# Block-sparse attention and a feed-forward layer on one core: first batch with fixed keys and fixed v blocks used from one place, sampled keys copied for both halves of the heads at once, and the third tile's neighbour blocks loaded from memory

## Chip, core, metric

The kernel runs on 1 core of one Trainium2 chip. The metric is the device time of one execution in microseconds (us); lower is better. The kernel before was timed three times.

## What is computed

Four batches, 8 heads, 768 rows of 64 numbers; the rows lie in 24 blocks of 32. A block of queries sees its own block and its two neighbours, the first and the last block of the keys, and three sampled blocks. The first and the last block of queries see everything. A feed-forward layer follows, over all 3072 tokens of width 512. All is f32.

```python
def _attn_ref(q, k, v, sampled_blocks):            # q, k, v: 4, 8, 768, 64
    scores = scale * np.matmul(q, k.transpose(0, 1, 3, 2))
    mask = np.abs(blk_i - blk_j) <= 1
    mask = mask | (blk_i == 0) | (blk_j == 0) | (blk_i == n_blocks - 1) | (blk_j == n_blocks - 1)
    for qb in range(n_blocks):
        for kb in sampled_blocks[qb]:
            mask[qb * block:(qb + 1) * block, kb * block:(kb + 1) * block] = True
    scores = np.where(mask, scores, -1000000000.0)
    ...
    return np.matmul(attn, v)

def _moe_ref(x, w_in, w_out):                      # 3072 x 512, 512 x 2048, 2048 x 512
    h = np.maximum(x @ w_in, 0.0)
    return h * h @ w_out
```

## The kernel before

A **tile** is 128 rows of queries (4 blocks) of one batch: 24 tiles, numbered k = 0 to 23, six a batch (t = 0 to 5). Three tiles make a **chunk**; the feed-forward layer works on a chunk at a time (`moe`), while the attention of the next chunk runs between its matmuls. The first chunk (k = 0, 1, 2) has no such partner: its attention is all there is in the first 58 us, and we call this stretch **the start**. `moe(0)` begins when the three tiles of x are done: `turn` turns them (tile xt), casts (xh, on ACT) and takes the rest (xl, on DVE), and the first product of the layer is ph<-xh,WI (L788).

The attention is cut into units. A `Half` is one tile and half of the heads (u = 0 or 1): `scores` (tile s, L374), `maxima` (m, DVE, L385), `exps` (p, ACT, L423), `turn` (pt, PE, L437), `copies` (pT, ACT, L446), `values` (pv, PE, L459) and `norm` (x, DVE, L474 to L479). A `Whole` does the first and last block of queries of a batch for a pair of heads (tiles g, mg, pg, ptg, pTg, pvg, in the same steps). In the start there are 4 wholes and 6 halves, put in by `units` one every STEP_0 = 5 steps, and a table of lags (LAG_0) says how many steps lie between two parts of a unit. Every engine then works through its own list in this written order, and an instruction that waits holds up all that stand behind it on its engine.

What a Half needs beside q:

- **Keys.** kn holds all keys of the batch for one half of the heads. KG holds, for one tile, the fixed blocks (first and last) and three sampled blocks for each of its four blocks of queries. For batch 0, POOL fills KG: `static_keys` (L284) one copy of 128x512 for each half, `copy_keys` (L263) 12 copies of 128x64 for each half. For later batches SP loads KG from memory.
- **v.** Each tile k < 3 has its own V[k]: V[k][0] holds on its first 64 rows the fixed blocks, four times over (once for each block of queries), and below them two sampled blocks; V[k][1] holds the third sampled block and the three neighbours. `load_sampled` (L317) brings the sampled blocks with 12 DMAs a tile on SP's queue. The fixed blocks are loaded once and copied five times (`copy_static`, L209, ACT). The neighbours of k = 0 are loaded; those of k = 1 and 2 are copied from vn, the batch's v (`copy_window`, L217, 24 copies of 32x260 a tile), on POOL, ACT and DVE.

SP's DMAs take eight semaphores in turn, so that one is issued only when the eighth before it has landed. On POOL's queue lie the loads of kn and vn and of the feed-forward weights (craw, L692, 512 KB each), AHEAD = 5 of them ahead of their use: the weights come as 64-bit numbers, and a `cut` (L708, L710 on ACT, L719, L720 on DVE) makes f32 of a craw.

```python
        if now >= FIXED_0 and fixed:
            f, *at = fixed.pop(0)
            f(*at, nc.scalar.copy)          # one ACT copy a step, from step 7 on
        if now >= CUT_0[0] and (now - CUT_0[0]) % CUT_0[1] == 0:
            cut_next()                      # one weight block every 5 steps, from step 30 on
```

## Time and profile before

| | us |
|---|---|
| time, median of 3 runs (758.05 to 761.56) | 760.67 |
| time of the profiled execution | 760.55 |
| its span, first to last instruction | 758.8 |
| attention of the first chunk until the first xh | 58.0 |
| busy in the span: PE / ACT / POOL / DVE | 732.4 / 539.7 / 502.3 / 499.8 |

The span is taken from one execution. Its own time is 1.75 us longer than the span; that part lies around the first and last instruction. A group line gives the line of the kernel, engine, operation, the tiles out<-in, the shape and the count, then busy time and mean ns of one, then the engine's idle time just before them and what ended it. In the timeline the columns are start, length (of all instructions in the row together), engine, line and operation. PEld is the loading of weights into TensorE; SPq and POOLq are DMA issues. The view of windows gives busy time of every engine in a stretch, then the granted TensorE clock, the busy share of the DMA engines and GB/s.

### The profile page before, as it was taken

The page shows a single profiled execution, that of the slowest core. Times are in us where ns is not written, and L with a number is a line of the kernel's source. Part 1 is how long each engine was busy: PE and PEld are TensorE (multiplying, and loading weights), DVE is VectorE, ACT ScalarE, POOL GpSimd, SP SyncE. Part 2 cuts the span into 40 slices and gives each one's busy share as a digit, 9 for nine tenths or more (in the row PEclk, how much of TensorE's full clock was granted, in tenths as well). Part 3 has the DMA queues.
Part 4 walks back from the last instruction along what each step waited for, and adds up shares of the span by engine and source line. Part 5 has one row for each costly group of instructions (what it writes and reads, how often), then busy time and mean ns, then how long its engine had stood idle before and what let it go on. Part 6 is the DMA issues. An engine that isn't in the chain of part 4 may idle for free.

```text
span 758.8 us, 26292 instructions
## 1 busy us (share of the span) xinstructions
PE 732.4 (97%) x9832; PEld 612.3 (81%) x9832; DVE 499.8 (66%) x987; ACT 539.7 (71%) x1193; POOL 502.3 (66%) x636
## 2 busy tenths in 40 slices
PE   4879999999999999999999999999999999999997
PEld 2656776668888888888888888887888888888986
DVE  5785785658785756667777575666868666645452
ACT  5896877798876876789786767679876776733222
POOL 6963844227776675757767567666876575777885
PEclk9799999999999999999999999999999999999999
DMA  8776799544543536544434344655344352201001
GB/s 283 224 215 172 228 264 344 130 117 131 140 114 93 146 86 176 153 109 128 113 105 106 101 126 109 221 120 140 79 124 118 75 143 64 51 1 44 1 1 41
DMA packets 92290, 97.45 MB, mean 128 GB/s; under 512 B 14787, under 2 KB 79428, under 8 KB 92164
## 3 DMA queue, kind: packets, MB, share of 16 engines
q1 hardware_dynamic: 86036, 72.41, 37.1%
q0 software_dynamic: 5696, 22.58, 9.2%
q8 instruction: 78, 1.28, 0.7%
q10 hardware_dynamic: 432, 0.79, 0.3%
q14 instruction: 48, 0.39, 0.2%
HBM read 89.43 MB, written 6.29 MB: 126 GB/s over the span
## 4 chain that ended last, share of the span: by engine, by line
PE 85%; ACT 5%; DMA 4%; DVE 4%; issue 1%; SPq 1%; ACTq 0%; POOL 0%; DVEq 0%; POOLq 0%
PE ph L788 33%; PE po L826 30%; PE s L374 7%; PE pv L459 5%; PE po L816 4%; PE g L546 2%; PE pvg L604 2%; DMA V<-in_v_dram 2%; DMA KG<-in_k_dram 1%; PE xt L773 1%; PE pt L437 1%; DVE xl L777 1%; ACT V L209 1%; DMA kn<-in_kn_dram 1%; SPq L317 1%
## 5 line engine op out<-in xcount | busy, mean ns | idle before, releaser
L413 ACT ACTIVATE pm<-p 32x256 f32<-32x256 f32 x576 | 239.2, 415 | 13.2 <-DVE p L391 4.8
L788 PE MATMUL ph<-xh,wi 128*128 128x384 f32 x832 | 237.8, 347 | 0.0
L826 PE MATMUL po<-wo,gh 128*128 128x512 f32 x672 | 213.8, 399 | 0.0
L755 POOL TENSOR_TENSOR wi<-W,wi 128x512 fp32r<-128x512 f32 x104 | 142.3, 1368 | 68.4 <-DVE wi L754 35.2
L806 POOL TENSOR_TENSOR gl<-gf,gh 128x384 fp32r<-128x384 f32 x112 | 117.4, 1048 | 93.0 <-DVE gf L804 80.6
L755 POOL TENSOR_TENSOR wo<-WO,wo 128x512 fp32r<-128x512 f32 x112 | 145.9, 1302 | 49.5 <-DVE wo L754 48.5
L792 ACT ACTIVATE r<-ph 128x384 f32<-128x384 f32 x128 | 63.0, 492 | 161.3 <-PE ph L788 156.1
L804 DVE SCALAR_TENSOR_TENSOR gf<-ph,r 128x384 f32<-128x384 f32 x112 | 62.3, 556 | 150.3 <-ACT r L792 136.4
L788 PEld LDWEIGHTS ph<-xh,wi 128*128 128x128 f32 x832 | 150.4, 188 | 13.4 <-issue 7.4
L826 PEld LDWEIGHTS po<-wo,gh 128*128 128x128 f32 x672 | 123.5, 188 | 23.0 <-issue 2.8
L788 PE MATMUL ph<-xl,wi 128*128 128x384 f32 x416 | 141.4, 340 | 0.0
L826 PE MATMUL po<-wo,gl 128*128 128x512 f32 x336 | 133.2, 396 | 0.0
L754 DVE CAST wo<-WO 128x512 fp32r<-128x512 f32 x112 | 84.4, 753 | 0.0
L788 PEld LDWEIGHTS ph<-xl,wi 128*128 128x128 f32 x416 | 78.2, 188 | 6.9 <-issue 2.9
L826 PEld LDWEIGHTS po<-wo,gl 128*128 128x128 f32 x336 | 63.1, 188 | 15.7 <-POOL gl L806 1.0
L385 DVE TENSOR_REDUCE m<-s 128x2 f32<-128x512 f32 x96 | 61.6, 683 | 11.2 <-PE s L374 10.9
L799 ACT ACTIVATE gh<-r 128x384 fp32r<-128x384 f32 x112 | 59.0, 526 | 9.3 <-ACT r L792 0.4
L459 PEld LDWEIGHTS pv<-V,pT 128*32 128x32 f32 x3072 | 47.7, 110 | 19.8 <-issue 9.5
L459 PE MATMUL pv<-V,pT 128*32 128x65 f32 x3072 | 56.2, 223 | 5.0 <-ACT pT L446 4.8
L788 PE MATMUL ph<-xh,WI 128*128 128x384 f32 x192 | 54.4, 344 | 0.8 <-ACT xh L776 0.8
L374 PE MATMUL s<-KG,q 64*32 64x160 f32 x1536 | 51.2, 305 | 1.4 <-issue 1.0
L418 DVE STREAM_TRANSPOSE pT<-pm 128x1024 f32<-128x1024 f32 x36 | 44.6, 1239 | 4.9 <-ACT pm L413 4.7
(85 smaller groups left out, 933.0 us busy)
## 6 DMA issues: line engine op xcount, KB each, us to landing
craw<-in_w_dram POOLq DMA_DIRECT2D x32, 512.0 KB, 5.9
V<-in_v_dram SPq DMA_DIRECT2D x504, 32.5 KB, 1.8
KG<-in_k_dram SPq DMA_DIRECT2D x216, 64.0 KB, 2.0
V<-in_v_dram SPq DMA_DIRECT2D x28, 390.0 KB, 4.5
q<-in_q_dram SPq DMA_DIRECT2D x24, 256.0 KB, 3.0
out_dram<-ot SPq DMA_DIRECT2D x21, 256.0 KB, 2.5
V<-in_v_dram SPq DMA_DIRECT2D x16, 292.5 KB, 4.2
vn<-in_vn_dram SPq DMA_DIRECT2D x5, 780.0 KB, 6.4
```

The source lines that it names most:

```text
L374: nc.tensor.matmul(self.sb[e][j * BLK : (j + 1) * BLK, i * NSLOT + a : i * NSLOT + z], q[r, j, pr, :], k, start=True, stop=True,)
L385: nc.vector.tensor_reduce(m[:, e], self.sb[e].rearrange("p (i c) -> p i c", i=2), axis=AX, op=ALU.max)
L413: nc.scalar.activation(p[a * BLK : (a + 1) * BLK, j], x[j * BLK : (j + 1) * BLK, :, a], AF.Exp, scale=SCALE)
L459: nc.tensor.matmul(po[j * BLK : (j + 1) * BLK, h * VW : (h + 1) * VW], self.pT[:, j, 2 * e + i, c], v[:, self.u, j, hv : hv + VW], start=( ...
L754: nc.vector.tensor_copy(w[:, 0], src)
L755: nc.gpsimd.tensor_tensor(w[:, 1], src, w[:, 0], op=ALU.subtract)
L788: nc.tensor.matmul(ph[:, :TOK], w, x, start=(i == 0), stop=(i == len(steps) - 1))
L792: nc.scalar.activation(r, ph[:, :TOK], AF.Relu)
L799: nc.scalar.activation(gh, r, AF.Square)
L804: nc.vector.scalar_tensor_tensor(gf, ph[:, :TOK], 0.0, r, op0=ALU.max, op1=ALU.mult)
L806: nc.gpsimd.tensor_tensor(gl, gf, gh, op=ALU.subtract)
L826: nc.tensor.matmul(acc[c][u], g[:, at], w[:, k], start=(f == 0 and i == 0), stop=(f == NF - 1 and i == 2))
```

## The change

Five things, all for the first batch.

1. **Fixed keys from one place.** KG of tiles in batch 0 holds the sampled blocks alone. The scores against the first and last block are taken straight from the keys, for all 128 queries of the tile in one matmul per head (128x64). For this q is laid out so that a head's 128 queries lie side by side. `static_keys` is gone for these tiles.
2. **Fixed blocks of v from one place.** A tile `fixed` (64 rows, both halves) is loaded once. In `values` of tiles k < 3 one matmul per head multiplies it for all 128 queries; the sampled part of V[k][0] is multiplied from row 64 down. The six ACT copies of `copy_static` are gone; for tile 3 the fixed blocks are loaded (64x4x260, two DMAs). The turned p (pT) is laid out so that a head's 128 columns lie side by side.
3. **Both halves at once.** The keys lie in one tile KN and v in one tile VN; a sampled block is copied for both halves by one POOL copy (128x128), but for tile 0. Neighbour blocks of tile 1 are copied for both halves by one copy (32x2x260): 8 on POOL, 4 on ACT, none on DVE.
4. **Third tile.** The neighbours of tile k = 2 are loaded from memory by two DMAs, ahead of its sampled blocks on SP's queue.
5. **Order.** STEP_0 is 4, with new lags; the first half of tile 0 stands after two wholes instead of four; `values` of the start take their PSUM bank from the other pool; AHEAD is 4.

```diff
-AHEAD = 5
+AHEAD = 4
-STEP_0 = 5
+N_0 = 1
+STEP_0 = 4
+FROM_MEMORY = (2,)
-LAG_0 = {"s": 2, "x": 2, "t": 3, "c": 2, "v0": 2, "n": 2}
+LAG_0 = {"s": 3, "x": 2, "t": 3, "c": 1, "v0": 3, "n": 2}
-FIXED_0 = 7
-ON_ACT = 12
+FIXED_0 = 22
+ON_POOL, ON_DVE = 8, 0
...
-        copy(V[k][1][(1 + n) * BLK : (2 + n) * BLK, i, j], st["vn", b, i][r : r + BLK, blk // NJ])
+        copy(V[k][1][(1 + n) * BLK : (2 + n) * BLK, :, j], st["vn"][r : r + BLK, :, blk // NJ])
...
-        for u in range(2):
-            if t < UC:
-                static_keys(b, t, u, nc.gpsimd.tensor_copy)
-            kn = st["kn", b, u]
+        for us in (slice(0, 1), slice(1, 2)) if t == 0 else (slice(0, 2),):
             for j in range(NJ):
                 for r in range(NRAND):
                     nc.gpsimd.tensor_copy(
-                        kg[:, j, 2 + r, 2 * u : 2 * u + 2].unsqueeze(1), kn[:, bass.ds(vals[NRAND * j + r], 1)]
+                        k5[:, j, r, us].unsqueeze(2), KN[:, us, bass.ds(vals[NRAND * j + r], 1)]
                     )
...
+                for e in range(2 if b == 0 else 0):
+                    r = slice(e * D, (e + 1) * D)
+                    to = self.sb[e][:, i * NSLOT : i * NSLOT + S_RAND]
+                    nc.tensor.matmul(to, q[r, pr].rearrange("p j s -> p (j s)"), kn[r, 0 : NBLK : NBLK - 1, i, :], start=True, stop=True)
...
+            for e, i, at in heads:
+                h = e, i, at
+                if e:
+                    self.products(po, h, 0, VA, 2 * BLK, True, False)
+                    self.products(po, h, 1, VB, 0, False, False)
+                p = self.pT[0 : 2 * BLK, 2 * e + i, 0].rearrange("p j q -> p (j q)")
+                nc.tensor.matmul(po[:, at], p, st["fixed"][:, self.u, at], start=e == 0, stop=e == 1)
+                if e == 0:
+                    self.products(po, h, 1, VB, 0, False, False)
+                    self.products(po, h, 0, VA, 2 * BLK, False, True)
...
-                if self.t == NT - 1:
+                if self.t in (0, NT - 1) and (self.t or self.b == 0):
                     load_static(n, self.u)
...
+            whole = wholes[:2] + halves[:N_0] + wholes[2:] + halves[N_0:]
+            return [(i * STEP_0, u) for i, u in enumerate(whole)]
...
+    st["fixed"] = rot.tile([P, NT, HW // 2], F32, tag="vn", name="fixed", bufs=1)[0 : 2 * BLK, 0:2]
+    nc.sync.dma_start(st["fixed"].rearrange("p u c -> p (u c)"), vd[0, V_STATIC * BLK :])
+    for k in FROM_MEMORY:
+        load_window(k, None)
```

What this does to the engines' lists is seen at three places. ACT's list from its first exponential on (names end in whole or tile, half and a number of the buffer; pg, pTg belong to wholes, p and pT to halves, V to tiles' v). Before:

```order
L562 ACTIVATE pg_0_443<-g_0_0_434,mg_0_438 128x512
L562 ACTIVATE pg_0_443<-g_0_1_435,mg_0_438 128x256
L209 COPY V_78<-V_78 64x780 x2
L209 COPY V_122<-V_78 64x1040
L592 COPY pTg_0_466<-ptg_0_0_451 128x512
L562 ACTIVATE pg_1_469<-g_1_0_446,mg_1_459 128x512
L562 ACTIVATE pg_1_469<-g_1_1_447,mg_1_459 128x256
L209 COPY V_122<-V_78 64x1040
L209 COPY V_124<-V_78 64x1040 x2
L217 COPY V_125<-vn_0_133 32x260 x2
```

ACT's list of the changed kernel, from the second whole's exponentials to the four copies of neighbour blocks:

```order
L574 ACTIVATE pg_1_468<-g_1_1_408,mg_1_414 128x256
L604 COPY pTg_1_513<-ptg_1_0_501 128x512
L420 ACTIVATE p_0_0_474<-s_0_0_0_427,m_0_0_471 128x256 x2
L420 ACTIVATE p_0_0_474<-s_0_0_1_428,m_0_0_471 128x256 x2
L443 COPY pT_0_0_573<-pt_0_0_0_559 128x512
L443 COPY pT_0_0_573<-pt_0_0_1_560 128x512
L574 ACTIVATE pg_2_576<-g_2_0_509,mg_2_529 128x512
L574 ACTIVATE pg_2_576<-g_2_1_510,mg_2_529 128x256
L604 COPY pTg_2_704<-ptg_2_0_628 128x512
L574 ACTIVATE pg_3_707<-g_3_0_569,mg_3_586 128x512
L574 ACTIVATE pg_3_707<-g_3_1_570,mg_3_586 128x256
L211 COPY V_124<-VN 32x2x260 x4
```

The copies of V that stood between the wholes are gone; the first half's p and pT stand before the third whole, and the copies that are left stand behind the fourth whole's exponentials.

PE's list before, at the values of tile 0's first half (pv_0_0), which stand behind the scores of tile 1 (s_1_0):

```order
L374 MATMUL s_1_0_0_832<-KG_94,q_1_143 32x160
L374 MATMUL s_1_0_1_833<-KG_94,q_1_143 32x160
L459 MATMUL pv_0_0_868<-V_78,pT_0_0_815 32x65 x4
L459 MATMUL pv_0_0_868<-V_79,pT_0_0_815 32x65 x4
L459 MATMUL pv_0_0_868<-V_78,pT_0_0_815 32x65 x4
```

PE's list of the changed kernel at the same values:

```order
L616 MATMUL pvg_1_534<-VN,pTg_1_513 32x65 x24
L434 MATMUL pt_0_0_0_559<-ident,p_0_0_474 128x128 x4
L434 MATMUL pt_0_0_1_560<-ident,p_0_0_474 128x128 x4
L558 MATMUL g_3_0_569<-KN,QG 128x512
L558 MATMUL g_3_1_570<-KN,QG 128x256
L462 MATMUL pv_0_0_591<-fixed,pT_0_0_573 128x65
L472 MATMUL pv_0_0_591<-V_79,pT_0_0_573 32x65 x4
L472 MATMUL pv_0_0_591<-V_78,pT_0_0_573 32x65 x8
```

They now stand ahead of the third whole's turning, of the scores of tile 0's second half and of all of tile 1, and they read V_78 and V_79, into which the 12 sampled DMAs of tile 0 write.

SP's list before, from the last sampled DMA of tile 1 to the first ones of tile 2 (ISA rows are address arithmetic):

```order
L317 DMA V_123<-in_v_dram 32x2x260
L242 DMA q_2_219<-in_q_dram 128x512
L231 TENSOR_LOAD idx
L317 ISA
L317 DMA V_124<-in_v_dram 32x2x260
```

And of the changed kernel:

```order
L309 DMA V_124<-in_v_dram 32x2x260
L239 DMA q_2_217<-in_q_dram 128x512
L296 DMA V_126<-in_v_dram 96x4x260 x2
L228 TENSOR_LOAD idx
L309 ISA
L309 DMA V_125<-in_v_dram 32x2x260
```

Two DMAs of 390 KB have come in ahead of tile 2's sampled blocks. From the second batch on the lists of all engines are the same as before but for names.

More of the change, by code (lines that the diff above doesn't have):

```diff
@@ L195, in load_static, with copy_window @@
     def load_static(k, u, eng=nc.sync):
-        us = halves(k, u)
-        if us is None:
-            return
-        n = 1 if k == 0 else NJ
-        for i in range(us.start, us.stop):
-            src = columns(vd[order[k][0], V_STATIC * BLK :], i)
-            src = src.unsqueeze(1).broadcast_to([2 * BLK, n, HW // 2])
-            eng.dma_start(values_of(k)[0][0 : 2 * BLK, i, 0:n], src)
-    def copy_static(k, i, copy):
-        src = V[0][0][0 : 2 * BLK, i, 0:1]
-        dst = V[k][0][0 : 2 * BLK, i, 1 if k == 0 else 0 :]
-        copy(dst, src.broadcast_to(list(dst.shape)))
-    def copy_window(k, i, j, n, copy):
+        src = columns(vd[order[k][0], V_STATIC * BLK :], u)
+        src = src.unsqueeze(1).broadcast_to([2 * BLK, NJ, HW // 2])
+        eng.dma_start(values_of(k)[0][0 : 2 * BLK, u], src)
+    def copy_window(k, j, n, copy):
         b, t = order[k]
@@ L248, in keys_of @@
         st["kg", b, t] = (
-            own.tile([P, NJ, 2 + NRAND, NPAIR, BLK], F32, name=f"KG{k}") if own else KG[(k - (k >= UC)) % 2]
+            own.tile([P, NJ, NRAND, NPAIR, BLK], F32, name=f"KG{k}") if own else KG[(k - (k >= UC)) % 2]
         )
```

95 lines of the change are left out of this document (48 added, 47 removed).

## The prediction

> **What bounds the kernel now.** First the page's busy times, then the view of windows with the start (from ACT's first exponential to its last cut before xh) and the rest apart:
>
> ```profile
> PE 732.4 (97%) x9832; PEld 612.3 (81%) x9832; DVE 499.8 (66%) x987; ACT 539.7 (71%) x1193; POOL 502.3 (66%) x636
> 10.42:57.74 47.32, 35.90 (x1047) 27.62 (x1046) 36.48 (x99) 44.78 (x91) 37.92 (x137) 0.89 0.82 234
> 60.00:758.70 698.70, 691.16 (x8772) 581.46 (x8771) 457.41 (x867) 491.68 (x1098) 458.64 (x475) 1.00 0.44 118
> ```
>
> PE's 97% is an average of two stages. After 60 us PE is busy for 691 of 699 us: nothing else can end that stage sooner, and it moves as a block with its beginning. In the start PE is busy for 36 of 47 us, ACT for 44.78. So the start is ACT's, and the time changes by what the first ph moves. Its end, from the timeline:
>
> ```profile
> 55.21 1.25 ACT L446 COPY pT<-pt 128x512 f32<-128x512 f32 x2
> 56.03 1.38 PE L459 MATMUL pv<-V,pT 128*32 128x65 f32 x64 [0.97 <-ACT pT L446]
> 57.88 0.42 DVE L479 TENSOR_TENSOR x<-pv,rec 128x256 f32<-128x256 f32 x1
> 58.03 1.56 ACT L776 CAST xh<-xt 128x512 fp32r<-128x512 f32 x3 [0.29 <-PE xt L773]
> 59.64 0.44 PE L788 MATMUL ph<-xh,WI 128*128 128x384 f32 x1 [0.78 <-ACT xh L776]
> ```
>
> The last copies of pT end at 56.46, and 3.18 us later, through pv, norm, xt and xh, the first ph begins. What ACT does from 10.42 on, in groups:
>
> ```profile
> L217 ACT COPY V<-vn 32x260 f32<-32x260 f32 x24 | 9.7, 406 | 0.4
> L423 ACT ACTIVATE p<-s,m 128x256 f32<-128x256 f32 x24 | 9.7, 530 | 0.1
> L446 ACT COPY pT<-pt 128x512 f32<-128x512 f32 x12 | 7.0, 662 | 2.0 <-PE pt L437 1.9
> L710 ACT ACTIVATE craw<-craw,below 128x512 int32<-128x512 uint16 x6 | 5.2, 873 | 0.0
> L209 ACT COPY V<-V 64x1040 f32<-64x1040 f32 x4 | 4.0, 1062 | 0.0
> L562 ACT ACTIVATE pg<-g,mg 128x512 f32<-128x512 f32 x4 | 2.8, 688 | 8.4 <-DVE mg L555 8.4
> L592 ACT COPY pTg<-ptg 128x512 f32<-128x512 f32 x4 | 2.3, 583 | 0.1
> L708 ACT ACTIVATE W<-craw 128x512 f32<-128x512 f32 x3 | 2.3, 763 | 0.0
> L562 ACT ACTIVATE pg<-g,mg 128x256 f32<-128x256 f32 x4 | 1.9, 468 | 0.0
> L209 ACT COPY V<-V 64x780 f32<-64x780 f32 x2 | 1.6, 836 | 0.0
> ```
>
> **What ACT loses.** The six copies of fixed blocks: 4.0 + 1.6 = 5.6 us. The 24 copies of neighbours: 9.7 us. Four copies of 32x520 come in. No such copy is in the trace; it lies between 32x260 (0.41) and 64x780 (0.84), and I take the middle, 0.63, so 2.5 us. A step count from the new lags ends the start with five cuts instead of six: one cut (0.76 + 0.87, of which ACT overlaps some) is 1.3 us. In all 5.6 + 9.7 - 2.5 + 1.3 = 14.1 us. If nothing else stood in the way, the first ph would move by that much. It is the upper end of the gain.
>
> **What is late next: the sampled blocks of tile 0.** pv_0_0 now stands on PE ahead of the third whole's turning and of the second half's scores, and it needs all 12 sampled DMAs of tile 0. Its list before that is short: after the first ptg, at 12.1, come s_0_0, pvg, ptg, g, pvg, pt, g, and by the rows
>
> ```profile
> 11.25 0.85 PE L584 MATMUL ptg<-ident,pg 128*128 128x128 f32 x6 [0.37 <-ACT pg L562]
> 14.43 0.89 PE L604 MATMUL pvg<-vn,pTg 128*32 128x65 f32 x48 [1.00 <-ACT pTg L592]
> 15.96 1.46 PE L546 MATMUL g<-kn,QG 128*128 128x512 f32 x4
> 36.83 1.09 PE L437 MATMUL pt<-ident,p 128*128 128x128 f32 x8
> 84.74 1.14 PE s L374 x62
> ```
>
> they take 1.14 + 0.89 + 0.85 + 1.46 + 0.89 + 1.09 + 1.46 = 7.8 us. So PE stands at pv_0_0 at about 20. When is the data there? In SP's timeline and the DMA view (the last two rows are one DMA issued at 20.74, and the span of all those of L317 in the first 60 us):
>
> ```profile
> 8.21 13.10 SPq L317 DMA_DIRECT2D V<-in_v_dram  x12
> 17.85 2.18 POOL L263 COPY KG<-kn 128x64 f32 x12
> 19.98 2.61 POOL L692 DMA_DIRECT2D craw<-in_w_dram  x5
> V<-in_v_dram SPq DMA_DIRECT2D x1, 65.0 KB, 5.9
> DMA to landing us min/median/max: 2.2/4.5/9.8
> ```
>
> The twelfth was issued at 20.74 and landed 5.9 us later, at 26.6. Nobody minded: pv_0_0 ran at 34.9. The five craw loads share its way. In the changed kernel POOL has three copies of 0.61 less ahead of them, and its second dozen pairs become one dozen of 128x128 (0.18 for 64 elements, 0.61 for 512: about 0.25 each), so the loads, now four, go out at about 16.9 instead of 19.98. SP's pace up to the eighth DMA (17.7) stays, since it waits for landings of loads that are the same as before. So at about 19, when weights begin to flow, five of the twelve are still to come. How fast they go beside weights, in the DMA view from 22 to 30 us:
>
> ```profile
> q0 software_dynamic: 655, 2.41, 86.8%
> q1 hardware_dynamic: 406, 0.34, 14.4%
> ```
>
> q1 is SP's: 0.34 MB in 8 us are 5.1 DMAs of 65 KB, 1.56 us each. Five take 7.8 us, to 26.8. I take 26.7. Bounds: with the shortest landing of that row, 20.7 + 2.2 = 22.9; with the longest, 30.5. So a **new wait of PE of some 6.7 us**, for everything behind pv_0_0 on its list, takes the place of ACT's copies, and ACT runs dry behind it.
>
> The Trainium skill, "DMA: Bandwidth & Descriptors", section on queues, rings and completion order, states that each DMA engine takes turns between its queues packet by packet. The counts above (655 to 406, the latter 1 KB each) lean that way but are not equal; with strictly equal turns q1's five DMAs would be through sooner, by about 23, and that is the first rival below.
>
> **From the wait to the first ph.** Clock rows:
>
> ```profile
> 26.58:29.99 3.41, 1.22 (x50) 0.64 (x36) 3.20 (x11) 3.35 (x9) 3.27 (x11) 1.00 1.04 345
> 29.99:33.40 3.41, 2.83 (x42) 2.33 (x48) 3.16 (x12) 1.49 (x4) 3.41 (x18) 0.50 0.76 172
> 31.15 1.97 PE L437 MATMUL pt<-ident,p 128*128 128x128 f32 x8
> ```
>
> After 3.4 us with PE mostly idle the granted clock was 0.50, and eight transposes took 1.97 instead of 1.09 us. I expect the same behind the new wait. So from 26.7: two thirds of pv_0_0 and four transposes of ptg, 1.25 us at full clock, some 2.2 at half; ACT gets work at 28.9. The skill's page "TensorE: Matmul & The Clock Gate", part 1, gives the rule (about 3.4 us of idle bring half rate) and the row agrees; without it the time would be 1 us less.
>
> What ACT then does is compared with a stretch of before:
>
> ```profile
> 33.77 1.57 ACT L423 ACTIVATE p<-s,m 128x256 f32<-128x256 f32 x4
> ```
>
> From here (p of the second half) to the end of the last pT at 56.46 ACT took 22.7 us with five halves, seven neighbour copies, five cuts, a cast and its waits. The changed list from 28.9 on has the same five halves and cast, four cuts (-1.3), no such copies (-2.9), and in addition two pTg (0.58 each), one whole's exponentials (4.7 / 4 = 1.18) and the four wide copies (2.5), less the tenth by which such rows overlap on ACT (the groups above add up to more than 44.78): 4.45. That is 22.7 - 1.3 - 2.9 + 4.45 = 23.0, to 51.9. The tail of 3.18 us loses about 0.3, since pv now has 36 matmuls instead of 64 (1.38 us). First ph at about 54.8 instead of 59.64: **4.8 us less**.
>
> **Edits that I cost at nothing.** DVE was busy for 36.5 of the start's 47 us and loses all its neighbour copies. POOL was busy for 37.9 of them, and its copies of sampled keys for tiles 1 and 2 halve in number; they were hidden behind ACT, and stay so behind the wait. Were DVE as late as ACT, the cover would be gone, and each half's norm would add its own time; nothing in the rows says so. The two DMAs of fixed blocks for tile 3 fall into the stretch before 60, where the DMA engines have slack (0.82 busy). In the second chunk PE is the bound, and scores with 96 instead of 160 columns save at most 0.1 us of 1.14 for each of six halves; I count 0.3, inside the error. The sum goes against the profiled execution's own 760.55 (span 758.8; the rest lies outside), which is the median of the runs (760.67) to 0.12. 760.55 - 4.8 - 0.3 = **755.5 us**.
>
> **Rivals.**
>
> A, the wait is short (chance 0.15). The data lands at 22.9 and not at 26.7: 3.8 us more, **751.7**. For it: SP has one load fewer ahead, since one of the fixed blocks takes the place of two. Against it: the 5.9 us above.
>
> B, the third tile's data is late (0.25). Its neighbours come from memory, 0.8 MB ahead of its sampled blocks on SP:
>
> ```profile
> 35.36 10.22 SPq L317 DMA_DIRECT2D V<-in_v_dram  x12
> V<-in_v_dram SPq DMA_DIRECT2D x1, 65.0 KB, 3.2
> ```
>
> Before, the last was issued at 45.0 and landed at 48.2, and pv_2_0 came at 52.6. Now SP can be through with tile 1 some three us sooner, as the weights ahead of it are gone three us sooner, but it needs about 1 us for the two new issues, and 0.8 MB more take 2.3 us at the 2.75 MB in 8 us of the view above. So 45 to 49; pv_2_0 wants it at about 48. If it comes at 51, PE waits 3 us more: **758.5**, within 0.5%.
>
> C, slower (0.10). AHEAD = 4 takes one cut's time from the lead of every weight load, and in the stretch from 79 to 135 us the DMA engines are full:
>
> ```profile
> craw<-in_w_dram POOLq DMA_DIRECT2D x17, 512.0 KB, 6.1
> 89.08 1.11 POOL L692 DMA_DIRECT2D craw<-in_w_dram  x2
> 101.12 0.65 ACT L708 ACTIVATE W<-craw 128x512 f32<-128x512 f32 x1
> 105.77 0.65 ACT L708 ACTIVATE WO<-craw 128x512 f32<-128x512 f32 x1
> ```
>
> The second of these two loads had 11.5 us from issue to cut. A cut less is 3 us less, and the median landing is 6.1. If landings take 9 and more, each of 17 loads can hold PE for half a us or more: 8.5 to 10 us, and the time is about **765**. It decides from a landing of 8.5 us on, in most loads; before, the median was below that.
>
> **How the numbers follow.** Forecast 0.50 (752.5 to 758), A 0.15, B 0.25, C 0.10. The predicted time is the forecast's, 755.5. The range 750 to 760.5 leaves out part of C and the far end of the 14 us. A measurement of this kernel tells about 0.5%, 3.8 us, from no change; so faster means below 756.9. Four fifths of the forecast (0.40), A (0.15) and the early end of B (0.05) make 0.60; nearly all of C is slower, 0.09; the rest is 0.31.
>
> **What would show it.** Right: PE idle before pv_0_0 (its line in `values`) by 4 to 9 us, ended by a DMA of V; ACT dry in the same stretch and then full to the end; clock 0.50 behind it; first ph at 53 to 56; after it PE as before. A: that wait under 3 us. B: a second wait of PE, before pv_2_0, ended by a DMA of V. C: PE waits in ph or po after 75 us, behind ACT's cuts and craw. The forecast is wrong altogether if the first ph moves and the end doesn't.

## The result and the profile after

| | before | changed |
|---|---|---|
| median, us | 759.79 (758.05 to 761.56) | 784.57 (783.99 to 786.95) |
| ratio, 95% interval | | 1.0324 (1.0283 to 1.0365) |
| profiled execution, us (its span) | 760.55 (758.8) | 784.37 (782.6) |
| first ph begins, us | 59.64 | 80.45 |
| from there to the span's end, us | 699.2 | 702.2 |

24.8 us slower, where 5 us faster were forecast. Of the span's 23.8 us, 20.8 lie ahead of the first ph and 3.0 behind it. In this and the later tables the medians are of all executions, while the ratios leave out four that lay far above the others of their kernel at a lower granted clock: 1211.77 us in e2 (its profiled execution, at 0.557, so that e8's trace stands for it), 786.09 in e3, 793.54 in e7 and 777.89 in e18. First the page's busy line and the windows of the changed kernel (PE, PEld, DVE, ACT and POOL busy with their records, then granted clock, DMA share, GB/s): the start, the rest, one stretch of 10 us, and single windows of 3.41 us, on whose borders the granted clock changes.

```profile
PE 760.3 (97%) x9976; PEld 632.2 (81%) x9976; DVE 502.4 (64%) x975; ACT 527.6 (67%) x1167; POOL 485.7 (62%) x566
```

```profile
10.20:79.78 69.58, 60.88 (x1152) 45.06 (x1150) 31.92 (x89) 32.01 (x65) 24.63 (x78) 0.76 0.69 189
81.00:782.50 701.50, 695.18 (x8819) 584.91 (x8819) 465.34 (x869) 493.22 (x1099) 455.81 (x465) 1.00 0.43 118
...
60.00:70.00 10.00, 10.00 (x126) 7.43 (x126) 4.08 (x9) 3.83 (x8) 2.31 (x4) 0.50 0.91 265
...
55.94:59.35 3.41, 2.14 (x82) 1.47 (x77) 0.51 (x1) 3.41 (x8) 0.00 (x0) 1.00 0.26 55
59.35:62.76 3.41, 3.41 (x64) 2.42 (x61) 2.67 (x5) 0.04 (x1) 2.58 (x4) 0.50 0.47 125
62.76:66.18 3.42, 3.42 (x24) 2.67 (x25) 2.06 (x5) 1.50 (x4) 0.26 (x1) 0.50 0.99 308
...
76.42:79.83 3.41, 3.36 (x14) 2.84 (x14) 1.71 (x5) 1.19 (x3) 0.00 (x0) 0.50 0.00 0
```

ACT did lose its work: 32.0 us busy in the start instead of 44.8. But PE, 36 of 47 us before, is now busy for 61 of 70, and from 60 to 70 us for all ten, while ACT works for 3.8. PE is the bound now, and it runs on half the clock for 34 of these 70 us. PE's timeline shows the wait and the end of the start; the chain that ended last (its columns: start, length, engine, tile, line, records) shows one half's pv and, in the second chunk, one half's scores:

```profile
20.25 0.40 PE L462 MATMUL pv<-fixed,pT 64*128 64x65 f32 x2
...
25.14 0.39 PE L472 MATMUL pv<-V,pT 128*32 128x65 f32 x2 [4.25 <-DMA V<-in_v_dram]
28.50 1.38 PE L472 MATMUL pv<-V,pT 128*32 128x65 f32 x26 [2.97 <-DMA V<-in_v_dram]
...
80.45 0.45 PE L801 MATMUL ph<-xh,WI 128*128 128x384 f32 x1 [0.68 <-ACT xh L789]
```

```profile
45.58 0.36 PE pv L462 x2
45.94 0.86 PE pv L472 x32
46.81 0.59 PE pv L462 x4
47.39 0.87 PE pv L472 x32
48.26 0.36 PE pv L462 x2
...
107.83 0.37 PE s L360 x4
108.19 0.49 PE s L370 x32
108.69 0.37 PE s L360 x4
109.05 0.49 PE s L370 x32
```

At full clock a half's pv takes 3.04 us and its scores 1.72. The kernel before took 1.14 for the scores (its row stands in the prediction) and 1.05 to 1.43 for a pv at full clock; two in the stretch where PE is the bound:

```profile
77.01 1.27 PE pv L459 x64
...
89.35 1.05 PE pv L459 x64
```

So the full-width products (L462 in pv, L360 in the scores) don't save 0.3 us, they cost 1.8 us a half in pv (1.77 against the 1.27, 1.99 against the 1.05) and 0.6 in the scores. Six halves of scores lie behind the first ph: 6 x 0.58 = 3.5. Set side by side from the first ph on, the changed kernel has fallen 4.6 us further behind by the first scores of the second batch: these 3.5, and a window at half clock right behind the first ph (83.24 to 86.66). In those scores it gets 1.7 us back, since the kernel before stops there for 1.04 us. What is left at the end are the 3.0.

### The profile page after: what moved, and what is told of

It is laid out like the page before. It is cut to its first block, busy times and chain, and to the rows that moved or that the text cites. A ratio compares the mean times of both kernels' runs of the same rounds, so it can differ in the third digit from the quotient of the medians.

```text
span 782.6 us, 26414 instructions
## 1 busy us (share of the span) xinstructions
PE 760.3 (97%) x9976; PEld 632.2 (81%) x9976; DVE 502.4 (64%) x975; ACT 527.6 (67%) x1167; POOL 485.7 (62%) x566
## 4 chain that ended last, share of the span: by engine, by line
PE 91%; DMA 3%; DVE 2%; ACT 2%; SPq 1%; issue 1%; POOL 0%; ACTq 0%; POOLq 0%; DVEq 0%
PE ph L801 34%; PE po L839 29%; PE pv L472 7%; PE s L370 7%; PE po L829 5%; PE g L558 2%; PE pt L434 2%; PE pvg L616 2%; DMA q<-in_q_dram 2%; PE pv L462 1%; PE xt L786 1%; PE s L360 1%; DMA V<-in_v_dram 1%; DVE xl L790 1%; ACT pm L409 1%
## 5 line engine op out<-in xcount | busy, mean ns | idle before, releaser
L472 PE MATMUL pv<-V,pT 128*32 128x65 f32 (+1 forms) x3072 | 62.7, 228 | 7.2 <-DMA V<-in_v_dram 7.2
L472 PEld LDWEIGHTS pv<-V,pT 128*32 128x32 f32 (+1 forms) x3072 | 49.3, 112 | 24.5 <-issue 12.1
L370 PE MATMUL s<-KG,q 64*32 64x160 f32 (+1 forms) x1536 | 48.1, 290 | 0.4 <-ACT KG L278 0.2
```

The lines of the kernel that those rows point to most:

```text
L370: nc.tensor.matmul(self.sb[e][j * BLK : (j + 1) * BLK, i * NSLOT + a : i * NSLOT + z], q[r, pr, j], k, start=True, stop=True,)
L472: nc.tensor.matmul(po[j * BLK : (j + 1) * BLK, at], self.pT[r:, 2 * e + i, c, j], v[r:, self.u, j, at], start=start, stop=stop,)
```

## The experiments

Theories: **PE** (full-width products make PE the bound), **wait** (the early pv_0_0), **clock** (the half clock doubles what the others cost). All runs together, with the first ph of the profiled execution:

| run | median us | ratio to before, 95% | first ph |
|---|---|---|---|
| e1 without v's full-width products | 774.68 | 1.0194 (1.0140 to 1.0248) | 71.86 |
| e2 full-width ones grouped | 784.08 | 1.0279 (1.0219 to 1.0339) | see e8 |
| e3 no early half | 772.96 | 1.0120 (1.0042 to 1.0198) | 69.51 |
| e4 transposes in the wait | 784.29 | 1.0299 (1.0232 to 1.0367) | 79.77 |
| e5 fixed blocks as before | 763.29 | 1.0042 (1.0013 to 1.0071) | 61.85 |
| e6 the same, no early half | 759.62 | 0.9978 (0.9948 to 1.0009) | 59.28 |
| e7 more transposes | 790.95 | 1.0329 (1.0248 to 1.0410) | 86.72 |
| e8 grouped, no early half | 774.03 | 1.0181 (1.0120 to 1.0242) | 70.70 |
| e9 dense products added | 785.87 | 1.0329 (1.0273 to 1.0386) | 77.96 |
| e10 e6 with fewer products | 757.76 | 0.9960 (0.9931 to 0.9989) | 57.77 |
| e11 e6, weights later | 762.38 | 1.0012 (0.9988 to 1.0036) | 63.22 |
| e12 v's fixed blocks as before, no early half | 766.64 | 1.0068 (1.0040 to 1.0096) | 58.99 |
| e13 before without ACT's neighbour copies | 758.39 | 0.9977 (0.9947 to 1.0006) | 56.99 |
| e14 before with more code | 769.37 | 1.0132 (1.0074 to 1.0189) | 69.31 |
| e15 e6 in the old order | 763.45 | 1.0040 (1.0013 to 1.0068) | 62.51 |
| e16 before with wide pvg | 761.02 | 1.0026 (0.9995 to 1.0056) | 57.60 |
| e17 e6 with wide pvg | 761.71 | 1.0010 (0.9986 to 1.0034) | 62.80 |
| e18 grouped and sorted, no early half | 768.57 | 1.0157 (1.0099 to 1.0215) | 63.52 |

### Which part costs: e1, e3, e5, e6, e12

e1, in `values`, for the first chunk (cuts in the code are marked by ...; the flags start and stop of the products that are left move with it):

```diff
...
-                p = self.pT[0 : 2 * BLK, 2 * e + i, 0].rearrange("p j q -> p (j q)")
-                nc.tensor.matmul(po[:, at], p, st["fixed"][:, self.u, at], start=e == 0, stop=e == 1)
...
```

> The changed kernel without the four full-width products of v's fixed blocks per half in the first chunk (L462): that part of the sum is left out; everything else, the early wait too, stands. PE theory (the full-width products, which I had counted at nothing, make PE the bound behind the wait): pv of a half falls from 3.04 us to 1.1 to 1.4 at full clock, six halves give back 10 to 12 us and some of the half-clock stretch from 59 to 80 us; first ph at 58 to 66 instead of 80.45, time 763 to 772. Wait theory (the 7.2 us wait of pv_0_0 and what it does to the clock is the loss, PE's work is a side show): the wait and the half clock stand, first ph at 75 or later, time 778 to 784.

e3:

```diff
-N_0 = 1
+N_0 = 0
```

> The changed kernel with the first half behind all four wholes again (N_0 = 0), so that PE does not stand at pv_0_0 before its sampled blocks are there. Wait theory: all comes back, first ph at 60 or earlier, time 764 or less. PE theory: only the wait (7.2 us) and the half clock behind it (25 to 39 us, some 5 us of lost work) come back, PE stays the bound up to the first ph, first ph at 68 to 74, time 772 to 778.

Each gave back some 10 us, neither all of it: both theories had a part. In e3 three executions of one kernel lay at 767.1, 772.2 and 773.8 us with a mean clock of 0.998, 0.988 and 0.987: the same instructions differ by 6.6 us, and the clock with them.

e5 puts the fixed blocks back into V and, but for the scores of tile 2, into KG; with them ACT gets its six copies back and POOL those of the fixed keys (e6 with N_0 = 0 as well, e12 with the part on v alone and N_0 = 0):

```diff
-                for e in range(2 if b == 0 else 0):
+                for e in range(2 if self.k == 2 else 0):
...
+            for h in heads:
+                self.products(po, h, 0, VA, 0, True, False)
+                self.products(po, h, 1, VB, 0, False, True)
...
+        if now >= 7 and statics:
+            f, *at = statics.pop(0)
+            f(*at, nc.scalar.copy)
```

> The changed kernel with fixed blocks per query block again, the early first half kept: v's fixed rows are copied on ACT into all three tiles (six copies of about 1.06 us), the fixed keys of tiles 0 and 1 (and so of the second chunk) into KG by POOL; only tile 2 keeps the full-width scores. PE theory: without the early wait's help from narrow products PE is no bound any more, the wait of 7 us stays with the half clock behind it; the run without v's full-width products had the first ph at 71.9, and the scores give back another 2: first ph at 66 to 70 if the half clock from 58 on stays, 60 to 64 if it goes. The second chunk gives back 3 us. Time 760 to 770. Wait theory: first ph not before 70, time over 770.

> As the run before it (fixed blocks per query block on ACT and POOL, tile 2 keeps the full-width scores), and the first half stands behind all four wholes again. What is left of the change: keys copied for both halves at once, four wide neighbour copies instead of 24, the third tile's neighbours from memory, one load less of lead. If the two parts taken out are the whole loss, ACT is the bound of the start again and has some 5 to 8 us less to do than in the kernel before: first ph at 52 to 57, time 751 to 757. If the rest of the change costs too (weights with a load less of lead, the third tile's data late), time 760 or more, with a wait of PE on V or on cuts.

> The changed kernel with only v's fixed blocks per query block (copied on ACT) and the first half behind the wholes again; all twelve halves of the first batch keep the full-width scores. Against the run with fixed keys per query block too (759.6 us): the scores cost 0.55 us a half more, 3.3 us in the second chunk and up to 2.2 us in the first, where PE has slack: time 762 to 766. If the fixed keys cost nothing (as I had predicted, 0.3 us saved): 759 to 760.5. Against the run with both (773.0): the rest, 8 to 11 us, is v's.

By ratios: with the early half the full-width products cost 1.0324 - 1.0042 = 2.8%, 21 us; without it 1.0120 - 0.9978 = 1.4%. The early half costs 0.6%, 5 us, where they are gone, and 2.0% where they are not: each makes the other dearer, though e3's wide interval leaves open by how much. The clock fits this: in the first 100 us of the profiled executions the half clock lasted 37.5 us in the changed kernel, 20.5 in e3, and 6.8 in both e5 and e6. Of the 1.4% the keys have 1.0068 - 0.9978 = 0.9; the rest would be v's, but the intervals of e3 and e12 overlap, so that v's part without the early half is not shown. (e12's profiled execution, 762.08 us, was the fastest of its eleven; its first ph is no middle value.) e6 shows that the rest of the change costs nothing that can be measured, and gains nothing either: 751 to 757 were forecast. Why is the last group's question.

### What a full-width product costs: e2, e8, e18

e2 puts the four of a half ahead of the narrow ones (one accumulation over the whole bank), in the scores too; e8 is e2 with N_0 = 0:

```diff
+            for n, (e, i, at) in enumerate(heads):
...
+                nc.tensor.matmul(po[:, at], p, st["fixed"][:, self.u, at], start=n == 0, stop=False)
+            for n, h in enumerate(heads):
+                self.products(po, h, 0, VA, 2 * BLK, False, False)
+                self.products(po, h, 1, VB, 0, False, n == 3)
```

> The same matmuls, but the full-width ones of a half stand together: all four ahead of the 32-column ones, in pv and in the scores, so one change of shape per half in pv instead of four, and two instead of four in the scores, counting the way back. If the changes between shapes cost (the scores have no more columns to stream than before, and yet took 1.72 us instead of 1.14): pv falls from 3.04 to about 2.3 us, scores from 1.72 to about 1.4 at full clock; first ph 5 to 9 us earlier, a further 1.5 to 2 us in the second chunk, time 774 to 779. If the full-width matmuls cost by themselves: pv and scores stay within 0.2 us, time 782 to 787. Wait theory: no change either.

> The full-width products of a half grouped, and the first half behind the wholes again. Against the run with only the latter (773.0 us; pv 3.04 us at full clock): if the changes between the shapes cost, pv is 2.3 us and the scores 1.4 at full clock, and at equal share of half clock the time is 3 to 7 us less, 766 to 770. If the full-width products cost by themselves, pv and scores stay within 0.2 us and so does the time, 771 to 775.

The timeline of e8, one pv at full clock:

```profile
52.29 1.10 PE L460 MATMUL pv<-fixed,pT 64*128 64x65 f32 x8
53.33 2.06 PE L470 MATMUL pv<-V,pT 64*32 64x65 f32 x64
```

pv stayed at 3.03 us, the scores went to 1.52, the time did not move. But the narrow products took 2.06 us in the timeline here, against 1.12 to 1.49 there for a pv of the kernel before at full clock, with no wide one between them. They have two shapes: V[k][0] is now read from row 64 on (64x32), V[k][1] whole (128x32), in turns by head. Counting runs of equal shape, a pv has eight changes in the changed kernel and eight in e2: grouping had saved none. (The rows of PE's list in the part on the change show the alternation: after the wide product V_79 x4, then V_78 x8.) e18 sorts by shape, all of V[k][0] and then all of V[k][1], two changes:

```diff
...
+            for h in heads:
+                self.products(po, h, 0, VA, 2 * BLK, False, False)
+            for n, h in enumerate(heads):
+                self.products(po, h, 1, VB, 0, False, n == 3)
```

> As the grouped run without the early first half (774.0 us, pv 3.03 us at full clock), but the products of a half's pv are sorted into three runs by the part of the array that they occupy: the four of 64 rows by 128 columns, then all sixteen of 64 rows by 32, then all sixteen of 128 rows by 32. Counted again, the grouped kernel had as many changes between such shapes inside a pv as the changed one, eight (64x32 and 128x32 alternate by head), which is why grouping did nothing there; now there are two. Change theory, 0.1 us each (the run without the full-width products had four changes and 1.66 us, none cost 1.3): pv about 2.4 us at full clock, six halves give 3.6 us or more with the half clock, time 766 to 771. If not the changes but the kinds of products cost: pv stays at 2.9 to 3.1, time 772 to 776.

```profile
49.77 1.10 PE L460 MATMUL pv<-fixed,pT 64*128 64x65 f32 x8
50.80 1.26 PE L471 MATMUL pv<-V,pT 64*32 64x65 f32 x64
```

The same products took 0.80 us less with six changes less, 0.13 each. The median went from 774.0 to 768.6; the intervals of the two ratios overlap, so it is the pv that shows the saving and not the time. e1's pv, four changes and no wide product:

```profile
50.15 1.59 PE pv L470 x64
```

That is 0.08 a change over 1.27 and 0.14 over 1.05. In the scores two changes fewer saved 0.20, 0.10 each. So a change costs about 0.1 us, and of a pv's cost some 0.9 us are the four wide products themselves (2.2 us in e18, less its two changes and 1.05) and 0.8 to 1.1 the eight changes. The Trainium skill, "TensorEngine Tiling (Array Packing)", section Tiling Modes, says that changing the tiling mode drains TensorE; these rows agree and give the price.

### The granted clock: e4, e7, e9

e4 puts 64 transposes ahead of pv_0_0, e7 eight ahead of each of the six pv, e9 sixteen dense fp32r products ahead of each of the last three:

```diff
+            for _ in range(16 if self.name in ("0_1_1", "0_2_0", "0_2_1") else 0):
+                nc.tensor.matmul(po[:, 260:512], st["dense"][:, :P], st["dense"][:, :252], start=True, stop=True)
...
```

> The changed kernel with 64 transposes of 128x128 (some 7 us, into columns of pv_0_0's bank that nothing reads) put on PE ahead of pv_0_0, so that PE works while it waits. Idle theory of the clock: the granted clock stays 1.0 from 25 to 39 us, this stretch is some 5 us shorter, and the half clock from 59 to 80 stays or shifts; time 775 to 780, less if it goes too. If it is the kind of work behind the wait that holds the clock down and not the idle time: 0.50 comes from about 29 us on as before, and the time stays within 2 us of the changed kernel's 784.6. PE theory: in either case PE stays the bound and the first ph comes after 70.

> The changed kernel with eight more 128x128 transposes on PE ahead of each of the six pv of the first chunk (into columns of the bank that nothing reads; at full clock 1.1 us each time, 5.5 us on the path after pv_0_0). If the granted clock goes by how much of the array is used in a window of 3.41 us (so far full clock followed windows with over about 1450 columns of 128x128 equivalent, half clock those with fewer, PE 100% busy or not): the half clock from 59 to 80 us is gone or shorter, the three halves there take 5.2 us each instead of 6.8, and the first ph comes 1 to 5 us earlier although PE has more to do; time 779 to 783. If the clock goes by PE being busy, or by something outside PE: the added work is added, at half clock 2 us each time, first ph at 86 to 90, time 790 to 794.

> The changed kernel with sixteen dense products more (128x252, fp32r, into columns of the bank that nothing reads) on PE ahead of each of the last three pv of the first chunk: 48 products of about 0.11 us at full clock, 5.3 us in all, 10.6 at half clock. They add 4032 columns a half, in full-array columns. Array-use theory of the clock (a window of 3.41 us with under about 1500 full-array columns brings half clock, busy or not; the stretch from 59 to 80 us has 780 to 1284): each half then has some 6100 columns in 10 us even at half clock, over 2000 a window, so the clock comes back to 1.0 within a window or two; the three halves take 5.9 us each instead of 6.8, xt 1.5 instead of 2.8, first ph at 76 to 81, time within 4 us of the changed kernel's 784.6 or less although PE got 5.3 us more to do. If the clock does not follow the use of the array: 0.50 stays, first ph at 90 to 92, time 793 to 797.

e4 halved the first stretch of half clock (6.8 us instead of 13.7), but the second came as before, and the first ph moved by 0.7 us. e7 missed: the added work was simply added. Its expectation divided the columns of a half by its length at full clock; at half clock a half lasts 8.8 us (6.8 and eight transposes of 0.24), so its 3100 columns are 1200 a window, still too few. e9 adds 4000 in 2 us. Its timeline and windows:

```profile
58.70 2.13 PE L450 MATMUL pv<-dense 128*128 128x252 f32 x16
...
77.96 0.44 PE L803 MATMUL ph<-xh,WI 128*128 128x384 f32 x1 [0.78 <-ACT xh L791]
```

```profile
59.02:62.43 3.41, 3.41 (x54) 2.93 (x52) 2.59 (x5) 1.93 (x4) 1.40 (x1) 1.00 0.70 183
...
72.67:76.09 3.42, 3.42 (x77) 2.66 (x77) 0.30 (x2) 0.09 (x1) 0.00 (x0) 1.00 0.00 0
```

PE got some 6 us more to do and its first ph came 2.5 us sooner, with the clock at 1.00 where it had been 0.50. The profiled execution (781.98 us) was the fastest of four, whose median is 785.87: the kernel as a whole gained nothing, but it did 6 us more work in 1.3 us more time, and the mean clock of all four was 0.982 to 0.988, against 0.972 to 0.976 in the changed kernel. So e9 came out as the theory says: what keeps the clock is how much of the array works, and not PE being busy. e7, the other run that tried it ahead, did not, and its miss is explained only afterwards.

### Why less ACT brought nothing: e10, e11, e13 to e17

PE's timeline of e6, every stop of PE in the start for which the view names nothing that ended it ("issue"), then a wait in the second chunk; and from its DMA view of 20 to 60 us the queue of instructions (packets, MB, share):

```profile
29.42 0.65 PE L617 MATMUL pvg<-VN,pTg 128*32 128x65 f32 x13 [3.60 <-issue]
39.49 1.25 PE L473 MATMUL pv<-V,pT 128*32 128x65 f32 x34 [2.06 <-issue]
...
48.99 0.36 PE L378 MATMUL s<-KG,q 64*32 64x96 f32 x5 [0.45 <-issue]
53.91 0.43 PE L473 MATMUL pv<-V,pT 128*32 128x65 f32 x16 [1.00 <-issue]
...
134.35 0.33 PE L378 MATMUL s<-KG,q 64*32 64x160 f32 x2 [1.90 <-DMA KG<-in_k_dram]
```

```profile
q8 instruction: 8, 0.13, 1.5%
```

7.1 us of stops. They fall in the middle of runs of equal products, at PE's records 347, 598, 851 and 976, multiples of about 126 apart, and each ends 1.5 to 1.6 us after a packet of 16,384 bytes on that queue has landed (27.90, 37.93, 47.40, 52.27). So we take it that PE's code comes in blocks of 126 products with their weight loads. The kernel before has one such stop in the start, at record 347:

```profile
30.57 0.65 PE L604 MATMUL pvg<-vn,pTg 128*32 128x65 f32 x13 [1.74 <-issue]
```

That its other blocks came while PE waited for ACT anyway is likely, but not shown. e14 adds code to it and hardly any work, e13 takes ACT's copies away:

```diff
+            for n in range(21 if self.k < UC else 0):
+                at = slice(n % NJ * BLK, n % NJ * BLK + BLK)
+                nc.tensor.matmul(po[at, 300:301], ident[:, at], ident[:, 0:1], start=True, stop=True)
```

```diff
+    nc.vector.memset(V[2][1], 0.0)
...
-    fixed += windows[2, 0] + windows[2, 1][:ON_ACT]
```

> The kernel before, with 21 products of 32x32 by one column more (into a column that nothing reads) on PE ahead of each of the six pv of the first chunk: 252 PE records and as many weight loads, two blocks of code more, at some 7 to 25 ns a record 2 to 5 us of PE in all, where PE stands idle for 14 of 50 us. Code theory (in the start PE gets a block of 126 matmuls with their weight loads per 4 to 5 us): first ph 6 to 10 us later, at 66 to 70, time 766 to 770. ACT theory (PE has slack, ACT sets the pace): first ph at 59.5 to 62, time 759.5 to 762.

> The kernel before, without ACT's 24 copies of neighbour blocks for the third tile (9.7 us of ACT's 44.8 in the start); these rows stay zero, that part of the sum is left out, and nothing is loaded in their place. ACT theory (step 2 of the prediction: the start is ACT's, and what ACT loses moves the first ph): first ph 6 to 9 us earlier than 59.6, at 50.5 to 53.5, time 751 to 754. Rails theory (PE stops for its code behind 16 KB blocks, and ACT's copies lay in time that it would have spent waiting for PE): first ph at 57 to 60, at most 2.5 us earlier, time 757 to 760.5, and ACT idle where the copies stood, waiting for pt.

PE's timeline of e14, its last stops:

```profile
46.25 0.84 PE L462 MATMUL pv<-V,pT 128*32 128x65 f32 x42 [1.47 <-issue]
51.93 0.39 PE L454 MATMUL pv<-ident 128*32 128x1 f32 x27 [2.45 <-issue]
56.81 0.31 PE L454 MATMUL pv<-ident 128*32 128x1 f32 x17 [2.08 <-issue]
64.35 0.20 PE L454 MATMUL pv<-ident 128*32 128x1 f32 x3 [2.94 <-issue]
```

Two blocks of code, 252 records, cost 9.7 us of the first ph and 9 us of time. All such stops of its start add up to 11.8 us, against the 1.7 before: from record 600 on a block comes every 3.7 to 7.5 us. And in e13, ACT with 24 copies less, from its timeline, and PE's:

```profile
30.80 0.59 ACT L446 COPY pT<-pt 128x512 f32<-128x512 f32 x1 [5.35 <-PE pt L437]
```

```profile
56.99 0.44 PE L788 MATMUL ph<-xh,WI 128*128 128x384 f32 x1 [0.78 <-ACT xh L776]
...
132.27 0.33 PE L374 MATMUL s<-KG,q 64*32 64x160 f32 x2 [2.37 <-DMA KG<-in_k_dram]
```

9.7 us of ACT's work gone, and it waits for PE instead: the first ph moved by 2.65 us, the time by less than the interval tells. What the start did gain met the next rail, as we call a limit that holds the time where it was when another is taken away: at 132 us PE waits for the sampled keys of the second batch, whose transfers follow each other through the full DMA engines (0.91 to 1.03 busy from 100 to 140 us in the kernel before); in e6, too, 1.90 us are lost there.

The others work on these rails. e10, in the first chunk's pv of e6:

```diff
             for h in heads:
-                self.products(po, h, 0, VA, 0, True, False)
-                self.products(po, h, 1, VB, 0, False, True)
+                self.products(po, h, 0, VA, 0, True, True)
```

> The run with fixed blocks per query block and no early first half (759.6 us; first ph at 59.3), with the products of the second kind of block columns (neighbours and the third sampled block) left out of the first chunk's pv: 32 PE records of 64 less a half, 192 in all, that part of the sum is left out. In that run PE stood still 7.1 us without a releaser, each time at a record whose number is a multiple of about 126, behind a packet of 16 KB on the queue of instructions: code theory, one such block of 126 matmuls per 5 us or so is what PE gets while the DMA engines are full, and 192 records are 1.5 blocks: first ph 6 to 8 us earlier, at 51 to 53, time 752 to 754. If PE's own work is what counts: 6 x 0.55 us, first ph at 55.5 to 57, time 756 to 758. If ACT's chain bounds the start: first ph at 58 to 60, time 758 to 760.

e11, in e6:

```diff
-    for _ in range(AHEAD):
-        cut_next()
...
     deque(copy_keys(0, 2, begin), 0)
+    for _ in range(AHEAD):
+        cut_next()
```

> The same run (fixed blocks per query block, no early first half), with POOL's first four weight loads behind the eight neighbour copies, some 5 us later, so that the DMA engines are less full while the code blocks and the sampled blocks of v come in. Code theory: the stop of 3.6 us at the 347th record is under 1.5, the first ph comes 1 to 3 us earlier, time 756 to 758.5, unless the cuts of weights, first used at about 38, now wait for their loads. If PE's stops have nothing to do with the load on the DMA engines: they stay, and the time stays within 1 us of 759.6.

e15, in e6:

```diff
-AHEAD = 4
+AHEAD = 5
...
-STEP_0 = 4
+STEP_0 = 5
...
-LAG_0 = {"s": 3, "x": 2, "t": 3, "c": 1, "v0": 3, "n": 2}
+LAG_0 = {"s": 2, "x": 2, "t": 3, "c": 2, "v0": 2, "n": 2}
```

> The run with fixed blocks per query block and no early first half (759.6 us), with the lead of the weights (5), the step (5) and the lags of the kernel before: what is left of the change are the copies of keys for both halves at once, the 12 wide copies and the third tile's neighbours from memory. If the order and the lead cost what the relieved ACT had gained: time 752 to 757. If the start is bound by something that neither touches (code, the chain pt, pT, pv of PE and ACT): 758.5 to 760.5.

e16 in the kernel before, e17 in e6 (with `norm` reading the other head's columns further right):

```diff
+            for kt in range(NT if b == 0 else 0):
+                a, h = kt * P, pr % 2 * 2 * VW
+                nc.tensor.matmul(
+                    po[:, : 2 * VW], self.pT[:, a : a + P], vn[:, kt, h : h + 2 * VW], start=(kt == 0), stop=(kt == NT - 1)
+                )
...
```

> The kernel before, with pvg of the four wholes of the first batch as six products of 128 columns by 130 (both heads of a pair at once, the half that belongs to the other head is not read) instead of 24 of 32 columns by 65: 12 PE records instead of 48 each, 144 records less in the start, 1.1 blocks of code; PE itself works about as long (6 x 0.22 = 1.3 us instead of 0.89). Code theory alone: first ph up to 5 us earlier. Both-rails theory (code and ACT's copies each hold the start at about 59 us): ACT's 44.8 us stay, so at most 1 to 3 us: first ph at 56.5 to 59, time 757 to 760. If code is no bound in this kernel: PE has 1.6 us more to do, time 759.5 to 762.

> The same wide pvg in the run with fixed blocks per query block and no early first half (759.6 us), where ACT has 8 us less to do. Both-rails theory: with code and ACT both relieved the start moves: first ph at 54 to 57, time 754 to 757, faster than both kernels. If something else holds the first ph at 59 (the half clock, sampled blocks of v, the chain through pt, pT and pv): 758.5 to 761.

e10: 1.5 blocks of code less gave 1.5 us, not 6 to 8; waits for q, for ACT and for DVE took their place (in its profiled execution, the slowest of ten). e11 missed: the stop at record 347 did shrink, from 3.60 to 0.85 us, but the stops add up to 7.1 us again, at other records, and V's sampled blocks came 3.8 us late. e15: 9.5 us of stops, and no gain. e16: the profiled execution ran at clock 1.00 up to its last microseconds and the first ph came at 57.60, but the time is not better. Set beside the kernel before from the first ph on, it loses 1.9 us, spread evenly over products before which neither trace has a wait; e17 loses 1.8 us in the same way against e6. Both were run on a chip that no other experiment used, so this loss need not belong to the edit; the median stays the answer. e17: no gain either, with 4.5 us of stops and 2.5 of waiting for V. No version beat the kernel before beyond its interval, save e10, which leaves work out. So ACT's work, PE's code, v's sampled blocks and the keys at 132 us each appear as a rail in one run or another, and taking one away shows the next. That these four are all, and that they are equally long, is not shown.

## Why the prediction was wrong, point by point

1. **PE-bound after 60 us, moves as a block**: half right. From first ph to end 699.2 us before, 702.2 after; the scores of the second chunk alone add 3.5. And a start that is 0.4 us (e6) or 2.7 us (e13) sooner loses 1.90 or 2.37 us at 132 us.
2. **The start is ACT's, its 14.1 us are the most that can be gained**: the sum was nearly right (44.8 us busy less 14.1 are 30.7, and 32.0 were measured, in a longer start; the fixed blocks are six copies, as its group lines have it, and not five), its use wrong. ACT's busy share was high because its copies filled time in which PE's work was not ready; e13 took 9.7 us away and gained under 2, which its interval does not tell from nothing.
3. **The new wait of pv_0_0**: right in place, cause and size: PE came at 20.25 (20 forecast), data at 28.5 (26.7, bounds to 30.5), 7.2 us of wait (6.7), half clock behind it. The half clock was sized at 1 us and lasted 13.7; but e4, which halved it, gained only 0.7.
4. **Behind the wait ACT's list decides, first ph at 54.8**: this is the step that failed, by its two smallest terms. "pv now has 36 matmuls instead of 64" mixed two units: 64 are records, two for each fp32 product, of 32 products; the 32 all stay (their lower rows hold the sampled blocks) and four come in. And "save at most 0.1 us of 1.14" took the columns streamed for the cost. Measured at full clock: +1.77 us a pv and +0.58 a half's scores, 10.6 us in six pv and 2.9 in the five halves of scores that stand between the wait and the first ph. That made PE the bound, and the clock went with it: 20.5 us at half from 59 to 80. With the products taken out again but the wait kept (e5), the first ph came at 61.85 instead of 80.45: 18.6 of the 25.65 us by which 54.8 was missed. The other 7.05 are not taken apart; in e5 PE has 4.1 us of stops that no wait explains, and ACT has its six copies again. (One slip in the sum is small: 4.84 us less a tenth are 4.36, not 4.45.)
5. **Edits at nothing**: the third tile's data from memory was in time (PE waits for no V behind pv_0_0), and after 81 us the view of waits has 2.0 us of PE in all, 1.7 of them where the kernel before waits just as long, and never for cuts or craw (rivals B and C did not come; A neither).
6. **Slower** stood as a rival with a chance of 0.10, with a mechanism that did not occur. The cost of the products that the change adds had no bound from both sides; the trace held no 64x128 product beside narrow ones, so the sum should have kept a rival in which they don't overlap.

## What to carry to other kernels

Count what a change adds on the engine that isn't the bound, in the units of the trace, and price a new shape of instruction as a rival, not as a rounding term: a mixed order of array shapes costs at each change, and a stretch of products that use little of the array can cost the clock as well. Before expecting a gain from relieving the busiest engine, remove its work outright in one run: if the end hardly moves, it was filling time. In a stage of many small products, look for stops that nothing in the view explains, at equal distances in the count of products: there the code itself may be the limit.

## What was not expected of the hardware

- **Clock.** In full-array columns (columns streamed times the share of rows and of columns that a product occupies, summed over PE's records in a window of 3.41 us), the windows of the changed kernel from 45.70 on have 1615, 1896, 1812, 1016, 780, 1284, 780, 1260, 804 and 1568. The clock of the window behind each is 1.0, 1.0, 1.0, then 0.5 six times, then 1.0. In e3 a window in which PE was busy throughout, with 1324, was followed by half clock:

```profile
38.10:41.51 3.41, 3.41 (x105) 2.50 (x90) 1.46 (x3) 2.05 (x5) 3.02 (x12) 1.00 1.12 271
41.51:44.92 3.41, 3.41 (x46) 2.68 (x48) 2.57 (x6) 2.12 (x5) 0.87 (x3) 0.50 0.83 233
```

  Counted so in 19 traces up to 85 us, windows under 1200 were all followed by half clock and, but for five, those over 1530 by full clock, with both outcomes in between. The five: one of e10 (1792), and the window with the first ph (2112 to 2272) in the changed kernel, e3, e4 and e18, each followed by a half one. Why is open. The two limits are read off these same windows. Since the products take about twice as long at half clock (eight transposes 1.97 us instead of 1.09), a window then holds about half the columns, and the state keeps itself. The Trainium skill, "TensorE: Matmul & The Clock Gate", part 1, gives one busy window of about 3.4 us as enough to release the clock; five windows with PE busy throughout did not (59.35 to 76.42), and there the measurement decides.
- **Code.** Blocks of 16,384 bytes, 126 products each; in every trace each stop of PE up to 70 us that the view puts down to "issue" ended 1.25 to 1.7 us after such a packet had landed. What sets the moment of its request was not tried.
- **Change of array shape.** About 0.1 us on PE (0.10 in the scores, 0.13 in e18's pv, 0.08 to 0.14 in e1's).
